# A scan's mixing products and the splitting of its result in two halves, a unit apart in every block; two sums of w_out in another place

## The chip, the cores and the metric

The kernel runs on one core of a Trainium2 chip. The metric is the device time of one execution in microseconds. Smaller is better. The engines are named as the profile names them: PE is TensorE (matmuls), PEld its weight loads, DVE is VectorE, ACT is ScalarE, POOL is GpSimd, SP is SyncE, which issues nearly all DMAs here.

## The reference

A chunked state space scan (4 sequences, 8 heads, 768 tokens, head width 32, state 16), and then a two-layer network with a hard-swish between the layers, over 3072 tokens of width 256, with 2048 hidden units:

```
y_intra = einsum('bhij,bhjd->bhid', (C B^T) * exp(cum_i - cum_j) * causal, x)
y_inter = einsum('bhin,bhnd->bhid', C, state) * exp(cum)
state   = decay_full * state + sum_j decay_from_j * B_j x_j
x2 = y, heads side by side                  # (3072, 256)
h  = x2 @ w_in                              # (3072, 2048)
g  = h * clip(h + 3, 0, 6) / 6
out = g @ w_out                             # (3072, 256)
```

The reference computes the scan in chunks of 32 tokens; the result does not depend on the length of a chunk.

## The kernel before

**Chunks and blocks.** The 768 tokens of each sequence are cut into six chunks of 128; chunk c of the scan gives the 512 tokens (128 of each of four sequences) of block c of the network. The network's block k runs on PE while the scan of chunk c = k + 1 is woven into it, so that chunk c is ready when block c begins. The loop over k at the end of the kernel writes this order out by hand; every engine works through its own queue in the order in which the code issues. Block 0's weights arrive and are decoded during block 0, which therefore has a form of its own (`mlp_in`, `first_out`).

**The network's block.** In blocks 1 to 5 the first product splits operands in three parts: `y` into `high`, `low` and `gap`, w_in into `w_high`, `w_low`, `w_gap`. For each of 16 slices f of the hidden units, `lead` (L687) multiplies `gap` by `w_gap` and has DVE (odd f, L696) or ACT (even f, L699) scale the result in PSUM; `follow` (L701) adds the products of `high` and `low`, and ACT (L706) and DVE (L707) make g of it. `lead` runs two slices ahead of `follow`, and six PSUM banks go round. The second product of blocks 1 to 4 is `wide_units` (L851), a scheme with seven products in place of eight for 2 x 2 quarters, in 14 units of work i = 0 to 13, two for each product. It needs sums of quarters of w_out, made once by `weight_sums` (L750, instructions L761), in the order t3, t2, t4 and t1, and sums of quarters of g, made in every block by POOL (`g_sums`, L769, instructions L779). Units 2 and 3 use t4, units 6 and 7 use t1, units 8 and 9 use t3, units 10 and 11 use t2. At unit 12 the first two `lead`s of the next block are issued. The last block's second product is `out_units`.

**The scan's chunk.** In the same units stand: `scores` (L529) and `multiply` (L573) at unit 2, which give the masked and decayed scores in `L` (DVE, L584), and the state in the middle of the chunk (`mid`); `renew` for the new state; `decay_ends` for the next chunk (ACT, L401, and POOL, L412). Then `results` (L937) issues `mix` (L598) and `split_y` (L666). `mix` multiplies scores by x: for each half u of the heads 64 products on 64 x 32 tiles of the array, each in two passes (128 matmuls for both halves, L610). To these `from_state` (L510) adds the state's part: for each of four sequences and four pairs of heads one product on a 32 x 64 tile, at tile position (32q, 64(q mod 2)) for pair q, in two passes (32 matmuls, L516). `split_y` copies y scaled to `high` (ACT, L671), takes `low` (DVE, L674) and `gap` (DVE, L677).

In which unit this happens depends on the chunk: for chunks 2, 4 and 5 all of it is in unit 6; for chunk 3 (`TURN`) the first half of the mixing is in unit 6, and the second half, the state's part of both halves and `split_y` are in unit 7. Chunk 1 has its place in the second product of block 0, where `first_out(b, i, c)` goes over quarters i of the hidden units and sequences b: scores behind (i, b) = (2, 3), results behind (3, 1), and the first two `lead`s of block 1 inside (3, 3). Chunk 0 is computed before the loop; there alone `from_state` is issued in two halves, for pairs 0 and 1 behind the first half of the mixing and for pairs 2 and 3 behind the second.

After `results` stand, in the same unit, the load of x for the next chunk (`load_x`), the exponential of its decays (`from_start`, ACT L405) and, where there is such a chunk, the loads of the decay rows of the one behind that (`rows`: two DMAs of `L` and four of `eto`, on SP's queue, where the output's stores queue too).

Of the kernel before, what the change touches and what calls it, by code (L numbers as in the profile page):

```python
# [9 lines left out]
FP32R = mybir.dt.float32r  # L10
# [4 lines left out]
ALU = mybir.AluOpType  # L15
# [6 lines left out]
def kernel(  # L22
# [24 lines left out]
    nc = tc.nc  # L47
# [7 lines left out]
    NK = DM // P  # L55
    PC = DM
    NQ = NH // 2
    Z = 2.0 ** -12
    UP = 1.0 + Z
    CUT = 1.0 - Z / 2  # L60
# [26 lines left out]
    TURN = 3  # L87
# [71 lines left out]
    def conceal_in(t, pattern):  # L159
# [26 lines left out]
        out=head, in_=head, pattern=[[-2 * N, NQ], [-N, 2]], compare_op=ALU.is_ge,  # L186
        fill=0.0, base=0, channel_multiplier=1)
    nc.gpsimd.affine_select(
        out=head, in_=head, pattern=[[2 * N, NQ], [N, 2]], compare_op=ALU.is_ge,
# [69 lines left out]
    low = pre[:G, 10, :2 * P]  # L259
# [76 lines left out]
    def y_tile(name, dtype):  # L336
        return att.tile([P, NK, TB], dtype, name=name, tag="y", bufs=3)

    yTs, states, mids, bTs, bss, tmps = {}, {}, {}, {}, {}, {}
    ys, cbs, sps, adds = {}, {}, {}, {}  # L340
# [169 lines left out]
    def from_state(c, a, pairs=range(NQ)):  # L510

        csT, state = bTs[c][2], (mids[c] if a else states[c - 1])
        for b in range(NB):
            for q in pairs:
                pair, d0 = slice(32 * q, 32 * q + 32), 2 * D * (q % 2)
                nc.tensor.matmul(  # L516
                    out=ys[c][a, q // 2][d0:d0 + 2 * D, b], lhsT=state[pair, b],
                    rhs=csT[pair, b, HALF[a]], start=(a == 0 and b == 0), stop=True,
                    tile_position=(32 * q, d0), skip_group_check=True)
# [78 lines left out]
    def mix(c, parts=range(2)):  # L598


        xt = xts[c]
        if 0 in parts:
            ys[c].update({
                (1, u): ps.tile([P, NB, HT], FP32, name="y2", tag=f"f{u}") for u in range(2)})
        for u in parts:
            for b in range(NB):
                for h in range(u * HU, (u + 1) * HU):
                    for a, rows in enumerate(HALF):
                        d0 = D * (h % HU)
                        nc.tensor.matmul(  # L610
                            out=ys[c][a, u][d0:d0 + D, b], lhsT=xt[rows, b * NH + h],
                            rhs=Ls[c][rows, b, h], start=(b == 0 and a >= min(c, 1)), stop=True,
                            tile_position=(a * HT, d0), skip_group_check=True)
            if c == 0:
                from_state(c, 1, (2 * u, 2 * u + 1))
        if c and 1 in parts:
            from_state(c, 1)

    def keep(c):

# [5 lines left out]
    def y_half(t, a, u):  # L626
        return t[:, u].rearrange("p (b i) -> p b i", b=NB)[:, :, HALF[a]]
# [20 lines left out]
    highs, lows, gaps, hs = {}, {}, {}, {}  # L648
# [14 lines left out]
            out=w_part(i, w_gap, j), in0=w_part(i, w_high, j), scalar=1.0 + 1.0 / Z,  # L663
            in1=first_in[i][:, j], op0=ALU.mult, op1=ALU.subtract)

    def split_y(c):  # L666

        highs[c], lows[c], gaps[c] = (y_tile(n, FP32R) for n in ("high", "low", "gap"))
        for u in range(NK):
            for a in range(2):  # L670
                nc.scalar.mul(y_half(highs[c], a, u), ys[c][a, u], CUT)  # L671
        for u in range(NK):
            for a in range(2):
                nc.vector.tensor_tensor(  # L674
                    out=y_half(lows[c], a, u), in0=ys[c][a, u], in1=y_half(highs[c], a, u),
                    op=ALU.subtract)
            nc.vector.scalar_tensor_tensor(  # L677
                out=gaps[c][:, u], in0=lows[c][:, u], scalar=-1.0 / Z, in1=highs[c][:, u],
                op0=ALU.mult, op1=ALU.add)

    def in_product(h, w, y, f, start=False):
        for j in range(NK):
# [250 lines left out]
    def rows(c):  # L933
        load_decay(c)
        load_eto(c)

    def results(c, parts=range(2)):  # L937
        mix(c, parts)
        split_y(c)

    def decay_ends(c, b):
        decay(c, b)
# [13 lines left out]
    parts = {i: decode(i) for i in range(2 * NP)}  # L956

    def weights(i, n):
        for _ in range(n):
            next(parts[i], None)  # L960
# [63 lines left out]
    for k in range(NC):  # L1024
        gTs[k] = ffn.tile([P, NF, TB], FP32, name="gT")
        c, ahead = k + 1, k + 2
        if k == 0:
            for f in range(NF):
                mlp_in(k, f)
                for i in weave.get(f, []):  # L1030
                    weights(i, 1)
                if f in (6, 8):
                    diff_exp(c, f // 2 - 3)
            load_bc(ahead)
            weights(NP + 1, 1)
            weights(NP + 3, 1)
            weights(NP + 2, 3)
            sums = weight_sums()
            for i in range(NP):
                for b in range(NB):  # L1040
                    first_out(b, i, c)
                    if (i, b) == (0, 0):
                        weights(NP + 3, 1)
                        weights(NP + 2, 1)
                        weights(NP + 3, 3)
                        rows(ahead)
                    elif (i, b) == (1, 0):
                        for j in range(NP - 1):
                            high_w(j)
                        for j in range(2):  # L1050
                            low_w(j)
                            gap_w(j)
                    elif (i, b) == (2, 0):
                        turn(c, 1)
                        wake(c)
                        turn(c, 0)
                        low_w(2)
                        gap_w(2)
                        high_w(NP - 1)
                        for p in range(2):  # L1060
                            conceal(ahead, p)
                    elif (i, b) == (2, 3):
                        scores(c)
                        multiply(c)
                        renew(c)
                        decay_ends(ahead, 0)
                        decay_ends(ahead, 1)
                        next(sums)
                        next(sums)
                    elif (i, b) == (3, 1):  # L1070
                        results(c)
                        next(sums)
                        decay_ends(ahead, 2)
                        load_x(ahead)
            rows(ahead + 1)
            continue
        for f in range(NF):
            if f == 0:
                if ahead < NC:
                    load_bc(ahead)  # L1080
                if 1 < k and c < NC:
                    carry(c)
                turns = turn_parts(c) if c < TURN else iter(())
            if f + 2 < NF:
                lead(k, f + 2)
            follow(k, f)
            if k == 1:
                if f in (0, 2):
                    low_w(NP - 1, f // 2)
                if f in (4, 6):  # L1090
                    gap_w(NP - 1, f // 2 - 2)
                if f in (1, 3):
                    decay(c, NB - 1, range(f // 2 * HU, (f // 2 + 1) * HU))
                if f == 3:
                    ends(c, NB - 1)
                    from_start(c)
                    carry(c)
            if f in (4, 8) and ahead < NC:
                conceal(ahead, f // 4 - 1)
            if f in (5, 7, 8):  # L1100
                next(turns, None)
            if f == 9 and c < TURN:
                turn(c, 1)
            if f in (4, 8, 12):
                g_sums(k, f // 2 - 2)
        for i, _ in enumerate((wide_units if c < NC else out_units)(k)):
            if i == 0:
                g_sums(k, NJ - 2)
                if k == 1:
                    next(sums)  # L1110
            if c < NC:
                if i == 1 and c == NC - 1:
                    own_banks(c)
                if i == 2:
                    scores(c)
                    multiply(c)
                    if c < NC - 1:
                        renew(c)
                if ahead < NC and 2 <= i < 6:
                    decay_ends(ahead, i - 2)  # L1120
                if i == 6 and c == TURN:
                    mix(c, (0,))
                if i == (7 if c == TURN else 6):
                    results(c, (1,) if c == TURN else range(2))
                    if ahead < NC:
                        load_x(ahead)
                        from_start(ahead)
                    if ahead + 1 < NC:
                        rows(ahead + 1)
                if i == 9 and TURN <= ahead < NC:  # L1130
                    turn_all(ahead)
                if i == 12:
                    lead(c, 0)
                    lead(c, 1)
# [30 lines left out]
```

## Time and profile before

| | |
|---|---|
| median of three runs | 349.99 us (347.1 to 352.08) |
| the profiled execution | 349.42 us |
| its span, first to last instruction | 347.7 us |
| mean granted clock of TensorE | 0.995 |
| PE busy | 335.3 us, 96% of the span |
| DVE, ACT, POOL busy | 220.1, 173.5, 141.5 us |
| first product, L683, matmuls | 51.8 + 50.7 + 50.3 us |
| mixing products, L610 | 9.8 us in 768 matmuls |
| state's part of y, L516 | 5.1 us (with `mid`) in 192 matmuls |
| sums of w_out, L761 | 1.21, 1.32, 1.21 and 2.22 us |

The span is the time from the first to the last instruction of the program on the core; the execution's own time is 1.7 us more. Rows of the profile give for each line of the code the busy time, the mean length of an instruction in nanoseconds, and the idle time of its engine just before, with what ended it; "issue" there means that no wait for a semaphore was seen. The ends of matmuls are modelled, so the pace of a stream of them is read from where the next ones start. In the timeline a row merges consecutive instructions of one kind and gives the start, the length and the count. In a table by stretches each engine has its busy time and the number of its instructions, and after them stand the granted clock of TensorE, the share of the DMA engines' time and GB/s.

### The profile page before, as it was taken

Reading aid. Unit: us, or ns where it says so; the run is one execution under the profiler, and the core shown is the slowest. Engines: PE = TensorE matmul, PEld = TensorE weight load, DVE = VectorE, ACT = ScalarE, POOL = GpSimd, SP = SyncE. Lnnn points to the kernel's source line nnn. Section 1 sums busy time; section 2 is a strip of 40 time slices with the busy share of each in tenths; the row PEclk is TensorE's granted clock in tenths of the full one; section 3 lists DMA queues with packets and bytes.
Section 4 is the critical chain, followed back from the end, with each engine's and each line's share of the span. In section 5 each row is a group of like instructions: output and inputs, shape, how many; then the busy total and the mean of one; then the engine's idle time right before and its main releaser. Section 6 shows DMA issues by size and latency. Waiting matters only on the chain.

```text
span 347.7 us, 8242 instructions
## 1 busy us (share of the span) xinstructions
PE 335.3 (96%) x3408; PEld 267.8 (77%) x3408; DVE 220.1 (63%) x357; ACT 173.5 (50%) x360; POOL 141.5 (41%) x139
## 2 busy tenths in 40 slices
PE   6799999998999999999999999999999979999996
PEld 2554458887778888888888888888887868888996
DVE  6689999988697648774448674438663332576011
ACT  4768888737874651663741663741662010565000
POOL 3300000291299913299512299510399100089500
PEclk9999999999999999999999999999999989999999
DMA  7898969106930066241047242051200000200000
GB/s 170 160 340 170 248 194 173 33 2 94 198 59 17 5 96 135 34 62 42 2 60 164 35 58 50 4 67 23 34 4 0 2 8 11 32 16 0 2 31 30
DMA packets 91605, 24.89 MB, mean 72 GB/s; under 512 B 84208, under 2 KB 87952, under 8 KB 91056
## 3 DMA queue, kind: packets, MB, share of 16 engines
q1 hardware_dynamic: 87184, 23.06, 34.5%
q10 hardware_dynamic: 4384, 1.31, 1.6%
q8 instruction: 26, 0.43, 0.5%
q14 instruction: 11, 0.09, 0.1%
HBM read 21.07 MB, written 3.29 MB: 70 GB/s over the span
## 4 chain that ended last, share of the span: by engine, by line
PE 89%; DVE 5%; DMA 3%; issue 1%; ACT 1%; SPq 1%; DVEq 0%
PE h L683 31%; PE wb L860 13%; PE wc L860 8%; PE h L635 8%; PE wa L860 8%; PE o L734 6%; PE oa L793 4%; PE ob L793 4%; PE y L610 2%; PE y L516 2%; PE cb L543 2%; DMA raw<-in_moe_w_in_dram 2%; DVE L L584 1%; DMA pairs<-in_C_dram 1%; PE y L555 1%
## 5 line engine op out<-in xcount | busy, mean ns | idle before, releaser
L707 DVE SCALAR_TENSOR_TENSOR gT<-gT,h 128x512 f32<-128x512 f32 x80 | 54.9, 687 | 32.1 <-ACT gT L706 29.3
L706 ACT ACTIVATE gT<-h,half_up 128x512 f32<-128x512 f32 x80 | 55.1, 690 | 33.3 <-PE h L683 33.1
L779 POOL TENSOR_TENSOR s<-gT 128x512 f32<-128x512 f32 x20 | 25.7, 1287 | 69.9 <-DVE gT L707 69.9
L683 PE MATMUL h<-gap,w_gap 128*128 128x512 f32 x160 | 51.8, 409 | 1.0 <-DVE gap L677 1.0
L683 PE MATMUL h<-high,w_high 128*128 128x512 f32 x160 | 50.7, 398 | 0.1
L683 PE MATMUL h<-low,w_low 128*128 128x512 f32 x160 | 50.3, 395 | 0.0
L699 ACT ACTIVATE h<-h 128x512 f32<-128x512 f32 x40 | 23.6, 589 | 31.3 <-PE h L683 31.3
L683 PEld LDWEIGHTS h<-gap,w_gap 128*128 128x128 f32 x160 | 29.9, 188 | 8.0 <-DVE gap L677 1.4
L683 PEld LDWEIGHTS h<-high,w_high 128*128 128x128 f32 x160 | 29.5, 188 | 8.6 <-DVE h L696 2.0
L683 PEld LDWEIGHTS h<-low,w_low 128*128 128x128 f32 x160 | 30.1, 188 | 7.2
L860 PE MATMUL wb<-s,w_out 128*128 128x256 f32 x128 | 32.0, 395 | 0.0
L401 ACT ACTIVATE L<-L,cum_n 128x64 f32<-128x64 f32 x128 | 31.6, 337 | 0.7 <-POOL L L162 0.7
L734 PE MATMUL o<-w_out,gT 128*128 128x256 f32 x128 | 28.7, 381 | 0.0
L696 DVE TENSOR_SCALAR h<-h 128x512 f32<-128x512 f32 x40 | 27.7, 692 | 1.2 <-PE h L683 1.2
L419 POOL TENSOR_TENSOR tmp<-state,eto 128x256 f32<-128x256 f32 x5 | 3.6, 716 | 60.5 <-ACT eto L405 60.3
L635 PE MATMUL h<-yT,w 128*128 128x512 f32 x64 | 27.7, 594 | 0.0
L860 PEld LDWEIGHTS wb<-s,w_out 128*128 128x128 f32 x128 | 24.7, 196 | 3.9
L779 POOL TENSOR_TENSOR s<-s,gT 128x512 f32<-128x512 f32 x20 | 26.9, 1343 | 1.6
L584 DVE TENSOR_TENSOR L<-L,cb 128x512 f32<-128x512 f32 x24 | 15.3, 682 | 19.1 <-PE cb L543 16.3
L734 PEld LDWEIGHTS o<-w_out,gT 128*128 128x128 f32 x128 | 24.1, 190 | 3.8 <-issue 0.5
L412 POOL TENSOR_TENSOR bs<-B,L 128x128 f32<-128x128 f32 x24 | 12.7, 542 | 33.0 <-ACT L L401 27.9
L779 POOL TENSOR_TENSOR gT<-gT 128x512 f32<-128x512 f32 x20 | 25.8, 1291 | 0.0
(141 smaller groups left out, 534.7 us busy)
## 6 DMA issues: line engine op xcount, KB each, us to landing
raw<-in_moe_w_out_dram SPq DMA_DIRECT2D x4, 1024.0 KB
L<-cum_d SPq DMA_DIRECT2D x8, 512.0 KB
xt<-in_x_dram SPq DMA_DIRECT2D x6, 512.0 KB
raw<-in_moe_w_in_dram SPq DMA_DIRECT2D x3, 1024.0 KB
out_dram<-back SPq DMA_DIRECT2D x128, 16.0 KB
eto<-cum_e SPq DMA_DIRECT2D x20, 64.0 KB
B<-in_B_dram SPq DMA_DIRECT2D x5, 256.0 KB
raw<-in_moe_w_in_dram ACTq DMA_DIRECT2D x1, 1024.0 KB
```

The lines of the kernel that those rows point to most:

```text
L401: nc.scalar.activation(Ls[c][:, b, h], Ls[c][:, b, h], AF.Exp, bias=cum_n[:, c, g:g + 1])
L584: nc.vector.tensor_tensor(out=Ls[c][:, :, hs], in0=Ls[c][:, :, hs], in1=cbs[c][q], op=ALU.mult)
L635: nc.tensor.matmul(out=h.rearrange("p r i -> p (r i)"), lhsT=first_in[f // FP][:, j, f % FP * P:(f % FP + 1) * P], rhs=yTs[k][:, j], start ...
L683: nc.tensor.matmul(out=h, lhsT=w[:, j, f * P:(f + 1) * P], rhs=y[:, j], start=(start and j == 0), stop=True, skip_group_check=True)
L696: nc.vector.tensor_scalar(out=h, in0=h, scalar1=-Z / UP, scalar2=None, op0=ALU.mult)
L699: nc.scalar.mul(h, h, -Z / UP)
L706: nc.scalar.activation(g, h, AF.Relu, bias=half_up, scale=UP * UP / 6.0)
L707: nc.vector.scalar_tensor_tensor(out=g, in0=g, scalar=UP, in1=h, op0=ALU.min, op1=ALU.mult)
L734: nc.tensor.matmul(out=o[:, b % 2], lhsT=gTs[0][:, f, b * P:(b + 1) * P], rhs=w_out[:, f], start=(f == 0 and b % 2 == 0), stop=True, skip_ ...
L779: nc.gpsimd.tensor_tensor(out=o, in0=p_, in1=q_, op=op)
L793: nc.tensor.matmul(out=bank[:, slot], lhsT=lhs[:, j], rhs=rhs[:, j], start=(clear and j == 0), stop=True, skip_group_check=True)
L860: nc.tensor.matmul(out=bank[:, slot], lhsT=lhs[:, j], rhs=rhs[:, j], start=(clear and j == 0), stop=True, skip_group_check=True)
```

## The change

- `from_state` for the second half of a chunk is issued in two halves, for pairs 0 and 1 and for pairs 2 and 3, in all chunks and not only in chunk 0, each behind its half of the mixing.
- `split_y` and `results` take one half u at a time.
- Chunks 2 to 5: half 0 (mixing, its state part, its part of `high`, `low` and `gap`) in unit 6, half 1 in unit 7. `load_x`, `from_start` and `rows` follow half 1 in unit 7; for chunk 3 they were there already.
- Chunk 1: half 0 behind (3, 0) of block 0's second product, half 1 behind (3, 1).
- Sums of w_out: before, t3 and t2 were issued behind (2, 3), t4 behind (3, 1) and t1 in unit 0 of block 1. Now t3 is issued behind (3, 1), t2 and t4 behind slices f = 10 and f = 12 of block 1's first product, and t1 in unit 0 as before.

```
@@ mix
-            if c == 0:
-                from_state(c, 1, (2 * u, 2 * u + 1))
-        if c and 1 in parts:
-            from_state(c, 1)
+            from_state(c, 1, (2 * u, 2 * u + 1))
...
-    def split_y(c):
-        highs[c], lows[c], gaps[c] = (y_tile(n, FP32R) for n in ("high", "low", "gap"))
-        for u in range(NK):
-            for a in range(2):
-                nc.scalar.mul(y_half(highs[c], a, u), ys[c][a, u], CUT)
-        for u in range(NK):
-            for a in range(2):
...
+    def split_y(c, u):
+        if u == 0:
+            highs[c], lows[c], gaps[c] = (y_tile(n, FP32R) for n in ("high", "low", "gap"))
+        for a in range(2):
+            nc.scalar.mul(y_half(highs[c], a, u), ys[c][a, u], CUT)
+        for a in range(2):
+            nc.vector.tensor_tensor(
+                out=y_half(lows[c], a, u), in0=ys[c][a, u], in1=y_half(highs[c], a, u),
+                op=ALU.subtract)
+        nc.vector.scalar_tensor_tensor(
+            out=gaps[c][:, u], in0=lows[c][:, u], scalar=-1.0 / Z, in1=highs[c][:, u],
+            op0=ALU.mult, op1=ALU.add)
...
-    def results(c, parts=range(2)):
-        mix(c, parts)
-        split_y(c)
+    def results(c, u):
+        mix(c, (u,))
+        split_y(c, u)
@@ block 0, second product
                         decay_ends(ahead, 0)
                         decay_ends(ahead, 1)
-                        next(sums)
-                        next(sums)
+                    elif (i, b) == (3, 0):
+                        results(c, 0)
                     elif (i, b) == (3, 1):
-                        results(c)
+                        results(c, 1)
                         next(sums)
@@ first product of blocks 1 to 5
+            if k == 1 and f in (10, 12):
+                next(sums)
@@ units of the second product
-                if i == 6 and c == TURN:
-                    mix(c, (0,))
-                if i == (7 if c == TURN else 6):
-                    results(c, (1,) if c == TURN else range(2))
+                if i in (6, 7):
+                    results(c, i - 6)
+                if i == 7:
                     if ahead < NC:
                         load_x(ahead)
                         from_start(ahead)
```

More of the change, by code (lines that the diff above doesn't have):

```diff
@@ L664, in gap_w @@
             in1=first_in[i][:, j], op0=ALU.mult, op1=ALU.subtract)
-    def split_y(c):
-        highs[c], lows[c], gaps[c] = (y_tile(n, FP32R) for n in ("high", "low", "gap"))
-        for u in range(NK):
-            for a in range(2):
-                nc.scalar.mul(y_half(highs[c], a, u), ys[c][a, u], CUT)
-        for u in range(NK):
-            for a in range(2):
[L674 to L679, printed above, removed]
+    def split_y(c, u):
[10 more added lines that the diff above has]
+            op0=ALU.mult, op1=ALU.add)
     def in_product(h, w, y, f, start=False):
```

## The prediction

> **What bounds the kernel now.** I read the page first, then the chain of waits of PE, the stretches by block, and the timeline where PE stands still.
>
> ```profile
> PE 335.3 (96%) x3408; PEld 267.8 (77%) x3408; DVE 220.1 (63%) x357; ACT 173.5 (50%) x360; POOL 141.5 (41%) x139
> q8 instruction: 26, 0.43, 0.5%
> ...
> PE 89%; DVE 5%; DMA 3%; issue 1%; ACT 1%; SPq 1%; DVEq 0%
> ```
>
> PE sets the end: 89% of the last chain, 12.4 us of the span not busy. So a part of the change counts if it alters PE's own time or makes PE wait; work of DVE, ACT or SP counts only where PE runs into it. Blocks 1 to 4, from first output product to first output product, as stretches (length, then busy time and counts of each engine, clock, DMA):
>
> ```profile
> 108.65:160.20 51.55, 51.55 (x530) 43.03 (x529) 35.66 (x54) 25.62 (x64) 31.22 (x29) 1.00 0.37 60
> 160.20:212.13 51.93, 51.93 (x529) 42.99 (x529) 30.75 (x53) 25.62 (x64) 26.97 (x26) 1.00 0.36 60
> 212.13:263.70 51.57, 51.57 (x530) 43.01 (x529) 30.17 (x53) 25.62 (x64) 23.90 (x23) 1.00 0.18 27
> 263.70:319.40 55.70, 53.87 (x531) 44.32 (x530) 26.14 (x45) 17.67 (x31) 20.18 (x17) 0.97 0.07 11
> ```
>
> Three blocks run PE without a pause. The second, which alone splits the mixing already, is 0.37 longer than its neighbours (51.93 - 51.56). The last is 4.1 longer: it holds a pause and a spell of lower clock (0.97).
>
> **The pause in block 4, which the split should remove.**
>
> ```profile
> 280.20 0.69 PE L516 MATMUL y<-csT,mid 32*64 32x64 f32 x30
> 282.72 0.27 PE L516 MATMUL y<-csT,mid 32*64 32x64 f32 x2 [1.83 <-issue]
> ...
> 283.38:286.79 3.41, 3.41 (x10) 2.70 (x9) 1.47 (x3) 0.03 (x1) 0.00 (x0) 0.50 0.09 15
> ```
>
> PE stops before the last two of 32 products, and no semaphore is named ("issue"). The instruction queue q8 moved 0.43 MB in 26 packets, 16.5 KB each; PE's 6816 weight loads and matmuls over 26 are 262 a packet. Counting PE's instructions in the trace, this pause stands before number 6081 and the one at 20.29 us, also "issue", before number 705: 5376 apart, 21 times 256. So I read both as a packet of instructions that came late. Packet 23 started at 279.80 and took 1.47; PE had entered the preceding 256 at 279.01 and went on at 282.72: 3.71 from entering one page to having the next. Mixing plus state products are 320 instructions in 2.1 us, so a page that lies wholly in them is used up too soon. After the pause the clock is 0.50 for 3.41 us (third line), 1.70 lost. Block 4 against block 3 is 4.13 longer; 0.36 of that is that the old state's products stand in a unit of their own there (263.70 to 273.12 against 212.13 to 221.19, 9.42 against 9.06). The pause is thus worth 3.77. After the change a unit of `wb` (1.92) stands inside that page: the rest of the first mixing half 0.37, state half 0.61 (below), `wb` 1.92, second half 0.79, 13 of 32 state instructions 0.25, sum 3.94, over 3.71. I take -3.77; bounds 0 (the packet is later still: packet 10 started 3.07 after its page was entered) and -3.77.
>
> The Trainium skill, Runtime: NRT & Kernel Launch, section Instruction fetch mechanics, has it that the sequencer fetches 16 KiB (256 instructions) ahead and that crossing such a boundary is mostly hidden. The spacing agrees with the trace, the hiding doesn't (1.83 us). By that rule this part would bring nothing, and the sum below would be 355.3 in place of 351.5.
>
> **What the split costs PE.** Two prices, both already in the trace because chunk 0 and block 2 do them.
>
> ```profile
> 20.52 0.68 PE L516 MATMUL y<-csT,mid 32*64 32x64 f32 x16
> 21.13 0.86 PE L610 MATMUL y<-L,xt 64*32 64x64 f32 x64
> ...
> 124.79 0.69 PE L516 MATMUL y<-csT,mid 32*64 32x64 f32 x32
> ...
> 226.87 1.48 PE L610 MATMUL y<-L,xt 64*32 64x64 f32 x128
> 228.28 0.69 PE L516 MATMUL y<-csT,mid 32*64 32x64 f32 x32
> 228.90 1.99 PE L860 MATMUL wb<-s,w_out 128*128 128x256 f32 x8
> ```
>
> One more change from large to small products and back: block 2 shows it, 0.37. Blocks 1, 3, 4 and the end of block 0 get it anew: 4 x 0.37 = 1.48. The state products: chunk 0 issues them in two halves (pairs 0-1, then 2-3), and 16 instructions take from 20.52 to 21.13, 0.61; all 32 with four pairs take 124.79 to 125.41, 0.62. Two pairs use two tile positions where four use four, so a half takes as long as the whole. The change does this to chunks 1 to 5: 5 x 0.60 = 3.00. Bounds 0 (the halves stand between other products and might overlap them; in chunk 0 they don't) and 3.00; I take 3.00, the same line in the same form.
>
> **End of block 0.** Here DVE held PE up: `gap` of chunk 1 comes behind two sums of w_out (1.21 and 1.32).
>
> ```profile
> 82.44 0.53 PE L683 MATMUL h<-gap,w_gap 128*128 128x512 f32 x1
> ...
> 83.97 0.97 PE L683 MATMUL h<-gap,w_gap 128*128 128x512 f32 x3 [1.00 <-DVE gap L677]
> ```
>
> In a stream these products start 0.23 apart; here 1.53, so 1.30 is lost. With the sums gone, DVE is free at 78.4; ACT ends 16 exponentials (L401) at 79.30, then two `high` copies, the output copy (0.56), two more: 81.2. DVE then needs two `low` and a `gap` a half: first `gap` about 81.0, second 82.3. PE gets to them at 82.44 + 0.37 + 0.60 = 83.4. So -1.30, with 1.1 of cover; gone, it would give 1.30 back. The third sum then stands at 82.3 to 83.5, where the next scaling of h (L696) comes behind it as now.
>
> **The two sums in block 1's first product** (t2 and t4, behind the ramps of f = 10 and 12). DVE's order there now, and a sum beside POOL's:
>
> ```profile
> 103.30 0.69 DVE L707 SCALAR_TENSOR_TENSOR gT<-gT,h 128x512 f32<-128x512 f32 x1 [0.52 <-ACT gT L706]
> 103.91 0.69 DVE L696 TENSOR_SCALAR h<-h 128x512 f32<-128x512 f32 x1
> 104.70 0.69 DVE L707 SCALAR_TENSOR_TENSOR gT<-gT,h 128x512 f32<-128x512 f32 x1
> 106.10 0.69 DVE L707 SCALAR_TENSOR_TENSOR gT<-gT,h 128x512 f32<-128x512 f32 x1 [0.71 <-ACT gT L706]
> 106.71 0.69 DVE L696 TENSOR_SCALAR h<-h 128x512 f32<-128x512 f32 x1
> ...
> 110.02 2.22 DVE L761 TENSOR_TENSOR w_out<-w_out 128x1024 f32<-128x1024 f32 x1
> ...
> 111.23 2.13 POOL L779 TENSOR_TENSOR s<-s,gT 128x512 f32<-128x512 f32 x1
> ```
>
> Queued behind t2 is the L696 of f = 13, behind t4 that of f = 15, and PE's last products wait for that one: already now their weight load comes at 107.45, 0.05 after L696 ends, with a wait of 0.22. Inserted are 1.32 + 1.21 = 2.53; DVE has 0.71 + 0.11 free there (before 106.10, and before 104.70). So the last L696, and PE, are 1.71 late: the lower bound. Upper: POOL works without a break from 102.4 to 113.4, and t1, run against it, took 2.22 where its sisters took 1.21 to 1.32, while a POOL sum took 2.13 for 1.28. With 2.22 each: 4.44 - 0.82 = 3.62. A sum may arrive at any point of a POOL instruction, t1 came at the start of one, so I take the middle, 2.7.
>
> The Trainium skill, SBUF — State Buffer, section Who interferes with whom, speaks against this move: a DVE instruction with two SBUF inputs and a GpSimd one that reads SBUF exclude each other for a whole instruction. The t1 row agrees. By the rule at its worst the sum would be 352.4; without it, 350.5.
>
> **At nothing.** `high`, `low` and `gap` come in the same number; the first half is ready earlier, and the products that read them start some 5 us after the second (127.8 to 128.4 `gap`, 135.7 lead). In blocks 1 and 3 the load of x, the exponential of eto and the seven loads of the decay rows issue one unit (some 2.5) later; SP's output stores queue behind them, but x and the decays are read tens of us later, and only the last block's stores, which don't move, touch the end. POOL's sums shift by about 1 to 2; PE reads the last of them (the s of `wb`) 8 us after they are done.
>
> **The sum.** -3.77 + 1.48 + 3.00 - 1.30 + 2.7 = +2.1. On the profiled execution's 349.42 (span 347.7 and 1.7 around it) that is 351.5. That execution lies 0.6 under the median of the runs, 349.99.
>
> **Rivals.** (a) The late page stays late, though the change separates the halves. For: packets started between 0.7 and 3.1 after their page was entered. Against: 3.94 against 3.71, and no window of 256 instructions over the new order is shorter than about 3.8. It gives 351.5 + 3.8 = 355.3. (b) The slower side: semaphores added or taken shift the boundaries by a few instructions, and scores, 320 instructions in 2.4 us, run dry instead (their page 9 arrived about when it was needed: its packet ended at 114.27, PE came at 115.48). Each such pause costs 3.8; with the kept one of block 4 one more gives 359.1. It decides from the second pause on. Against: scores don't change and the boundary lies there only in blocks 1 to 3. (c) The sums hide: if L696 of f = 13 and 15 weren't behind them, +2.7 falls away: 348.8. Against: the order of the queue.
>
> **How the numbers follow.** Forecast 0.50 (own range 350.5 to 352.4), (a) 0.15, (b) 0.15, (c) 0.17, and 0.03 for a gain that no row shows. The range 348.0 to 355.8 takes in the forecast, (c) and (a), 0.82. Over 2% (7 us, about what a measurement of this kernel can tell from no change) are slower: (b), 0.15; faster: 0.03; within: 0.82.
>
> **What would show it.** Right: no "issue" gap near 280 and clock 1.00 there; block 4 near 52.9; blocks 1 and 3 near 52.5, block 2 near 52.5; each half of L516 about 0.6; no wait of L683 for `gap`; PE waiting for L696 at the end of block 1's first product, 1.7 to 3.6. Wrong: an "issue" pause of over 1 us in blocks 1 to 4, halves of L516 at 0.3, or no wait for L696.

## The result, and the profile after

The changed kernel took 352.67 us (median of 12 executions, 351.2 to 356.22), the kernel before 347.9 (12 executions, 347.1 to 352.08): a ratio of 1.0122, 95% interval 1.0088 to 1.0155. It is slower by 1.2%, about 4.2 us by the ratio and 4.8 at the medians, and so within the 2% and the range of the forecast, just above the likeliest case's own range (350.5 to 352.4). The profiled execution of the changed kernel took 351.53 with a span of 349.8, 2.1 us longer than the profiled span before. So two numbers have to be told apart in what follows: 2.1 between two profiled executions, and 4.2 (4.8 at the medians) between the kernels. Differences in us between kernels are by the ratio below, unless the text says otherwise.

In the changed file the lines of the network stand a few numbers lower: L670 and L673 are L674 and L677 before, L679 is L683, L692 is L696, L703 is L707, L757 is L761, L775 is L779, L856 is L860. The stretches of blocks 1 to 4 (length, busy time and counts of each engine, clock, DMA):

```profile
111.11:163.62 52.51, 52.51 (x530) 43.60 (x529) 33.48 (x53) 25.73 (x64) 31.04 (x28) 1.00 0.35 57
163.62:216.16 52.54, 52.54 (x530) 43.54 (x529) 31.05 (x53) 25.85 (x64) 27.40 (x26) 1.00 0.36 61
216.16:268.66 52.50, 52.50 (x529) 43.51 (x529) 30.35 (x53) 25.83 (x64) 24.32 (x23) 1.00 0.17 26
268.66:321.53 52.87, 52.87 (x531) 43.53 (x530) 26.20 (x45) 17.78 (x31) 20.18 (x17) 1.00 0.07 11
```

All four blocks now run PE without a pause and at full clock. Blocks 1 to 3 were 51.55, 51.93 and 51.57 and are 0.96, 0.61 and 0.93 longer; block 4 was 55.70 and is 2.83 shorter. The timeline of PE where the pause had been:

```profile
283.75 0.86 PE L610 MATMUL y<-L,xt 64*32 64x64 f32 x64
284.54 0.68 PE L516 MATMUL y<-csT,mid 32*64 32x64 f32 x16
285.15 1.99 PE L856 MATMUL wb<-s,w_out 128*128 128x256 f32 x8
287.07 0.86 PE L610 MATMUL y<-L,xt 64*32 64x64 f32 x64
287.86 0.68 PE L516 MATMUL y<-csT,mid 32*64 32x64 f32 x16
```

Read from start to start: a half of the mixing (32 products in two passes each, so 64 instructions) takes 0.79, a half of the state products 0.61 (284.54 to 285.15, and 0.61 again at the second half), the unit of `wb` 1.92. PE's 6081st instruction is still inside the second state half, and nothing stops before it.

The end of block 0 (DVE) and the first products that need `gap` (PE):

```profile
80.53 0.69 DVE L673 SCALAR_TENSOR_TENSOR gap<-low,high 128x512 fp32r<-128x512 f32 x1
81.14 0.79 DVE L670 TENSOR_TENSOR low<-y,high 128x256 fp32r<-128x256 f32 x2
81.97 0.69 DVE L673 SCALAR_TENSOR_TENSOR gap<-low,high 128x512 fp32r<-128x512 f32 x1
...
83.48 1.29 PE L679 MATMUL h<-gap,w_gap 128*128 128x512 f32 x4
84.61 1.02 PE L730 MATMUL o<-w_out,gT 128*128 128x256 f32 x4
```

Both gaps are there 0.8 us and more before PE asks for them. From the first product with `gap` to the output products behind the two leads PE now takes 1.13 (83.48 to 84.61), before 2.34 (82.44 to 84.78): 1.21 gained. Those output products in the kernel before, and its first products of block 1's second product:

```profile
84.78 1.02 PE L734 MATMUL o<-w_out,gT 128*128 128x256 f32 x4
...
108.49 1.24 PE L860 MATMUL wa<-gT,w_out 128*128 128x256 f32 x5
```

In the changed kernel, in block 1's first product, DVE, PE and POOL:

```profile
103.72 1.96 DVE L757 TENSOR_TENSOR t<-t,w_out 128x1024 f32<-128x1024 f32 x1
105.59 0.69 DVE L692 TENSOR_SCALAR h<-h 128x512 f32<-128x512 f32 x1
...
107.39 1.86 DVE L757 TENSOR_TENSOR t<-w_out,t 128x1024 f32<-128x1024 f32 x1
109.18 0.69 DVE L692 TENSOR_SCALAR h<-h 128x512 f32<-128x512 f32 x1
...
106.34 0.73 PE L679 MATMUL h<-high,w_high 128*128 128x512 f32 x2 [0.72 <-DVE h L692]
109.92 0.73 PE L679 MATMUL h<-high,w_high 128*128 128x512 f32 x2 [1.45 <-DVE h L692]
110.95 1.24 PE L856 MATMUL wa<-gT,w_out 128*128 128x256 f32 x5
...
104.57 2.23 POOL L775 TENSOR_TENSOR s<-gT 128x512 f32<-128x512 f32 x1
108.13 2.25 POOL L775 TENSOR_TENSOR gT<-gT 128x512 f32<-128x512 f32 x1
```

Each sum is followed by a scaling of h, and each of these two scalings ends about 0.05 before the product of PE that names it as what it waited for. Beside both sums a POOL instruction takes 2.2 where its neighbours take 1.3. From the output products behind the two leads to block 1's second product the kernel before took 23.71 (84.78 to 108.49), the changed one 26.34 (84.61 to 110.95): 2.63 more, of which 2.17 are the two waits named in PE's rows; the rest lies in the starts around them.

### The profile page after: what moved, and what is told of

Read it like the earlier page. It is cut to its first block, busy times and chain, and to the rows that moved or that the text cites. A ratio compares the mean times of both kernels' runs of the same rounds, so it can differ in the third digit from the quotient of the medians.

```text
span 349.8 us, 8240 instructions
## 1 busy us (share of the span) xinstructions
PE 338.1 (97%) x3408; PEld 269.9 (77%) x3408; DVE 219.7 (63%) x357; ACT 174.4 (50%) x360; POOL 145.0 (41%) x139
## 4 chain that ended last, share of the span: by engine, by line
PE 91%; DVE 3%; DMA 3%; ACT 1%; SPq 1%; issue 0%; DVEq 0%
PE h L679 29%; PE wb L856 12%; PE wc L856 8%; PE o L730 8%; PE h L632 8%; PE wa L856 8%; PE oa L789 4%; PE ob L789 4%; PE y L516 3%; PE y L610 3%; PE cb L543 2%; DMA raw<-in_moe_w_in_dram 2%; PE y L555 1%; DMA pairs<-in_C_dram 1%; DVE t L757 1%; ACT gT L702 1%
## 5 line engine op out<-in xcount | busy, mean ns | idle before, releaser
L703 DVE SCALAR_TENSOR_TENSOR gT<-gT,h 128x512 f32<-128x512 f32 x80 | 54.7, 686 | 31.6 <-ACT gT L702 28.9
L775 POOL TENSOR_TENSOR s<-gT 128x512 f32<-128x512 f32 x20 | 26.7, 1334 | 64.1 <-DVE gT L703 64.1
L679 PE MATMUL h<-high,w_high 128*128 128x512 f32 x160 | 50.9, 399 | 2.3 <-DVE h L692 2.2
L679 PE MATMUL h<-gap,w_gap 128*128 128x512 f32 x160 | 51.5, 408 | 0.0
L679 PE MATMUL h<-low,w_low 128*128 128x512 f32 x160 | 50.3, 395 | 0.0
L679 PEld LDWEIGHTS h<-high,w_high 128*128 128x128 f32 x160 | 29.4, 188 | 11.3 <-DVE h L692 4.9
L679 PEld LDWEIGHTS h<-low,w_low 128*128 128x128 f32 x160 | 30.1, 188 | 7.2
L679 PEld LDWEIGHTS h<-gap,w_gap 128*128 128x128 f32 x160 | 30.0, 188 | 6.7
L419 POOL TENSOR_TENSOR tmp<-state,eto 128x256 f32<-128x256 f32 x5 | 4.9, 983 | 65.0 <-ACT eto L405 64.9
L856 PE MATMUL wb<-s,w_out 128*128 128x256 f32 x128 | 30.7, 382 | 0.0
L692 DVE TENSOR_SCALAR h<-h 128x512 f32<-128x512 f32 x40 | 27.6, 691 | 2.2 <-PE h L679 2.2
L775 POOL TENSOR_TENSOR s<-s,gT 128x512 f32<-128x512 f32 x20 | 26.9, 1345 | 1.6
L856 PEld LDWEIGHTS wb<-s,w_out 128*128 128x128 f32 x128 | 24.0, 190 | 3.5
L775 POOL TENSOR_TENSOR gT<-gT 128x512 f32<-128x512 f32 x20 | 26.6, 1330 | 0.0
```

The lines of the kernel that those rows point to most:

```text
L679: nc.tensor.matmul(out=h, lhsT=w[:, j, f * P:(f + 1) * P], rhs=y[:, j], start=(start and j == 0), stop=True, skip_group_check=True)
L692: nc.vector.tensor_scalar(out=h, in0=h, scalar1=-Z / UP, scalar2=None, op0=ALU.mult)
L703: nc.vector.scalar_tensor_tensor(out=g, in0=g, scalar=UP, in1=h, op0=ALU.min, op1=ALU.mult)
L775: nc.gpsimd.tensor_tensor(out=o, in0=p_, in1=q_, op=op)
L856: nc.tensor.matmul(out=bank[:, slot], lhsT=lhs[:, j], rhs=rhs[:, j], start=(clear and j == 0), stop=True, skip_group_check=True)
```

## The experiments

The question after the result was not where the time goes in the profile, which adds up, but whether each cause is the one named, and why the kernels differ by 2 us more than their two profiles. All ratios are to the kernel before, with executions of it on the same chip beside each.

| kernel | median us | ratio to before, 95% interval | profiled span |
|---|---|---|---|
| changed kernel | 352.67 | 1.0122 (1.0088 to 1.0155) | 349.8 |
| before, once more | 348.16 | 0.9995 (0.9962 to 1.0029) | 346.6 |
| before, chunk 5 split | 346.5 | 0.9942 (0.9904 to 0.9980) | 345.7 |
| before, state products in halves | 349.92 | 1.0052 (1.0021 to 1.0083) | 349.3 |
| before, sums moved | 349.99 | 1.0051 (1.0014 to 1.0088) | 348.4 |
| changed, state products whole | 349.5 | 1.0034 (0.9999 to 1.0070) | 347.8 |
| changed, sums put back | 349.33 | 1.0036 (1.0000 to 1.0073) | 347.6 |
| changed, POOL away from the sums | 352.84 | 1.0133 (1.0057 to 1.0210) | 349.4 |
| changed, state products woven in | 358.67 | 1.0301 (1.0257 to 1.0344) | 356.8 |
| before, three findings | 345.77 | 0.9912 (0.9879 to 0.9945) | 344.7 |

**The kernel before, once more.** No edit.

> The kernel before, unchanged, profiled once more. Theory: the pause of about 1.8 us late in block 4 is in every execution, since it comes from where PE's instructions lie, while the spell at half clock behind it (1.7 us) is in some only; so this execution shows the pause near 281 us, and where the clock stays at 1.00 a span near 346.0 against 347.7. Rival: the pause itself is a chance of the first profile; then no pause is seen and the span is near 344.

The pause is there, 1.30 us, at the same two products, with the clock at 1.00 all through block 4. From the chain that ended last, and the stretch of block 4:

```profile
281.40 0.62 PE y L516 x30
282.01 1.30 issue
283.32 0.27 PE y L516 x2
...
264.83:318.30 53.47, 52.16 (x530) 43.13 (x530) 26.11 (x45) 17.68 (x31) 20.21 (x17) 1.00 0.07 11
```

So the theory holds: the pause belongs to the program, the spell at half clock does not. Block 4 was 55.70 in the first profile and is 53.47 here. Of the four profiles that have this pause (the two of before, the halves and the moved sums) two show the spell in block 4 and two don't. The span came out at 346.6, not 346.0: chunk 0 had a pause of its own (1.2 us, "issue", before PE's 705th instruction; 0.47 in the first profile), and block 1 is 0.46 longer with an "issue" pause of 0.32 in its scores, while the pause in block 4 is 0.53 shorter.

**Chunk 5 split, nothing else.**

```
-                if i == 6 and c == TURN:
+                if i == 6 and c in (TURN, NC - 1):
                     mix(c, (0,))
-                if i == (7 if c == TURN else 6):
-                    results(c, (1,) if c == TURN else range(2))
+                if i == (7 if c in (TURN, NC - 1) else 6):
+                    results(c, (1,) if c in (TURN, NC - 1) else range(2))
```

> The kernel before, with chunk 5 alone taken as chunk 3 is: first half of the mixing in unit 6, second half, the undivided state products and the splitting of y in unit 7. Theory (a late instruction packet): one more unit of 1.9 us stands inside the packet's 256 instructions, the time from entering it to its end is 0.37 + 1.92 + 0.79 + 0.44 = 3.5 us against 3.7 needed, so the pause shrinks from 1.8 to 0.2 us or less and the clock stays at 1.00; the price is 0.37 for the switch of forms. Against a kernel before without the clock spell about 1.3 us faster, against one with it 3. Rival (the pause belongs to something else, such as a wait for mid or a bank): the pause stays and the time rises by 0.4 us.

```profile
265.15:317.43 52.28, 52.28 (x531) 43.00 (x530) 26.12 (x45) 17.56 (x31) 20.18 (x17) 1.00 0.07 11
```

No pause is left; block 4 is 1.19 shorter than in the profile just shown, the 0.37 for the split included. The pause is so worth 1.56 in the execution without the clock's spell and 3.79 in the one with it (53.47 and 55.70, each less 52.28 - 0.37). The 2.23 between them are 0.53 of a longer pause (1.83 against 1.30) and 1.70 of the spell. The kernel is faster than before by 0.6%, clear of its interval. A wait for mid or for a bank would have stayed, as no operand changed its producer.

**State products in halves, nothing else.**

```
-            if c == 0:
-                from_state(c, 1, (2 * u, 2 * u + 1))
-        if c and 1 in parts:
-            from_state(c, 1)
+            from_state(c, 1, (2 * u, 2 * u + 1))
```

> The kernel before, with the state products issued in two halves (pairs 0-1 behind the first half of the mixing, pairs 2-3 behind the second) in every chunk, all of it still in one unit. Theory: a half costs what the whole costs, so chunks 1 to 5 cost 0.6 us more each; in block 4 the longer section eats 0.6 of the pause, and block 1's gap waits are behind it by 0.6 less; so blocks 1 to 3 are 0.6 longer each, the whole about 1.8 slower. Rival: the halves overlap the mixing around them and the blocks keep their length within 0.1.

```profile
160.71:213.23 52.52, 52.52 (x529) 43.52 (x529) 31.23 (x53) 25.84 (x64) 27.41 (x26) 1.00 0.36 59
213.23:265.55 52.32, 52.32 (x529) 43.61 (x529) 30.16 (x53) 25.85 (x64) 24.36 (x23) 1.00 0.18 26
265.55:321.02 55.47, 54.62 (x530) 44.91 (x530) 26.14 (x45) 17.79 (x31) 20.19 (x17) 0.97 0.07 11
```

Block 2 is 0.59 longer; block 3 is 0.75 longer, since with both halves in one unit the mixing is cut as well (one change of form more; its price follows with the woven kernel). Block 1 (52.59) is 1.04 longer, of which 0.15 is a short pause in its scores. The rival is out. In block 4 the pause fell to 0.85, as the section is longer, and a spell at half clock stands behind it all the same, where none stands behind 1.30 in two other profiles; what brings the spell isn't shown. In time 0.5% slower, as expected.

**The changed kernel with the state products whole**, behind the first half of the mixing. For the second half of the heads they then open the sum:

```
@@ from_state
-                    rhs=csT[pair, b, HALF[a]], start=(a == 0 and b == 0), stop=True,
+                    rhs=csT[pair, b, HALF[a]], stop=True,
+                    start=(b == 0 and (a == 0 or (c > 0 and q >= 2))),
...
@@ mix
-                            rhs=Ls[c][rows, b, h], start=(b == 0 and a >= min(c, 1)), stop=True,
+                            rhs=Ls[c][rows, b, h], stop=True,
+                            start=(b == 0 and a >= min(c, 1) and (c == 0 or u == 0)),
...
-            from_state(c, 1, (2 * u, 2 * u + 1))
+            if c == 0:
+                from_state(c, 1, (2 * u, 2 * u + 1))
+            elif u == 0:
+                from_state(c, 1)
```

> The changed kernel, but with the state products undivided behind the first half of the mixing (for the second half of the heads they then open the sum, and the mixing adds to it). Theory: blocks 1 to 4 are 0.6 us shorter each, block 0's end too, where the cover of the gap shrinks from 0.8 to 0.2; in block 4 the packet has 0.37 + 0.62 + 1.92 + 0.79 less what lies behind its end, about 3.5, so a pause of up to 0.3 can come back. In all 2.7 to 3.0 us faster than the changed kernel. Rival: if halves cost nothing where they stand, the blocks keep 52.5.

```profile
111.52:163.42 51.90, 51.90 (x529) 42.99 (x529) 33.55 (x53) 25.72 (x64) 30.62 (x28) 1.00 0.36 58
267.29:319.56 52.27, 52.27 (x530) 43.00 (x530) 26.13 (x45) 17.66 (x31) 20.18 (x17) 1.00 0.07 11
```

Each block is 0.6 shorter than in the changed kernel (52.51 and 52.87), and no pause came back. Against before the ratio falls from 1.0122 to 1.0034, 0.9% or 3 us: the halves cost what they were said to cost.

**The state products woven into the mixing**, four behind each sequence's sixteen mixing products. This asks why a half is so dear.

```
@@ from_state
-    def from_state(c, a, pairs=range(NQ)):
+    def from_state(c, a, pairs=range(NQ), bs=range(NB)):
...
-        for b in range(NB):
+        for b in bs:
...
@@ mix, inside the loop over b and then behind it
+                if c:
+                    from_state(c, 1, (2 * u, 2 * u + 1), (b,))
-            from_state(c, 1, (2 * u, 2 * u + 1))
+            if c == 0:
+                from_state(c, 1, (2 * u, 2 * u + 1))
```

> The changed kernel, with the state products of each half issued sequence by sequence between the mixing products (four of each half's sixteen behind each sequence's mixing) and not behind them all. Theory: a half costs as much as the whole because its products use only two tile positions of the array and each waits for the one before at its position; with mixing products in between the positions have time to come free, so most of the 0.30 us that a half pays too much goes: blocks 1 to 4 become 0.3 to 0.6 us shorter each, the kernel 1.5 to 2.5 faster than the changed one. Rival: what a half pays too much is the change of form from mixing to state products and back; woven there are four of these changes in each half, and the blocks become longer.

The kernel becomes longer, as the rival said. The first half of one of its halves, from the chain that ended last:

```profile
126.99 0.27 PE y L610 x16
127.26 0.26 PE y L516 x4
127.52 0.27 PE y L610 x16
127.80 0.26 PE y L516 x4
```

A quarter of the mixing takes 0.27 where it took 0.20 (0.79 for four), and four state products 0.26 where they took 0.15. Instruction by instruction, PE's last matmul of one form starts at 235.017 and the first weight load of the other form at 235.161: 0.144 without a start, at each change of form. Within the state products the starts come in rounds of 0.058, two instructions a round with two pairs and four with four. So a half of 16 is 0.144 and eight rounds, the whole of 32 is 0.144 and eight rounds too, both 0.61. The theory had the rounds right and put the change of form at nothing; woven, a half has six changes more. Of the 0.60 that the two halves of the changed kernel pay over the whole, 0.144 is the one extra change, the rival's reason, and 0.46 the half-empty rounds, the larger part.

**The sums moved, nothing else** (t3 behind `results`, t2 and t4 behind f = 10 and 12):

```
-                        next(sums)
-                        next(sums)
...
+            if k == 1 and f in (10, 12):
+                next(sums)
```

> The kernel before, with the sums of w_out where the change puts them (t3 behind (3, 1) of block 0, t2 and t4 behind f = 10 and 12 of block 1's first product) and nothing else. Theory: the wait for gap at the end of block 0 goes (-1.3 us), DVE's two sums hold up the scalings behind them and PE waits 0.7 and 1.5 us (2.4 in all by the changed kernel's profile): 1.1 us slower, with the pause of block 4 as before. Rival: those waits come from the later arrival of the split halves, so without the split they aren't there and the kernel is 1.3 faster.

PE waits for the scalings 2.2 us in all, as in the changed kernel, though the mixing is not split here; the rival is out. The wait for `gap` did not go wholly: from the first product with `gap` to the output products behind it takes 1.41 (83.63 to 85.04), 0.28 more than in the changed kernel; here both gaps come behind one unit that holds all of the mixing. The time is 0.5% above before, 1.8 us, where 1.1 was expected. The profile adds up to 1.7: 0.93 gained there (2.34 to 1.41), 2.65 lost in block 1's first product (23.71 to 26.36).

**The changed kernel with the sums put back.** The same edit, reversed.

> The changed kernel, with the sums of w_out where they were before (t3 and t2 behind (2, 3), t4 behind (3, 1)). Theory: block 1's first product loses its waits (-2.4 us), and at the end of block 0 a wait of 0.4 to 0.6 for gap returns, less than the 1.0 of before since PE comes 1.0 later: about 1.9 faster than the changed kernel. Rival: if the sums only fill idle time of DVE in block 1, this kernel is slower than the changed one by the returned wait.

From the first `lead` to block 1's second product it takes 24.74 (84.05 to 108.79), in the changed kernel 27.28 (83.83 to 111.11). Of the wait for `gap` only 0.1 returns where 0.4 to 0.6 were expected; 1.17 us of DVE's time before `low` are idle in the changed kernel, and the sums fill these first. The ratio is 1.0036 in place of 1.0122.

**POOL away from the sums.**

```
-            if f in (4, 8) and ahead < NC:
+            if f in ((4,) if k == 1 else (4, 8)) and ahead < NC:
...
-            if f in (4, 8, 12):
+            if f in ((4,) if k == 1 else (4, 8, 12)):
                 g_sums(k, f // 2 - 2)
...
                 g_sums(k, NJ - 2)
                 if k == 1:
+                    conceal(ahead, 1)
+                    g_sums(k, 2)
+                    g_sums(k, 4)
```

> The changed kernel, with POOL's sums of g for f = 4 to 11 of block 1 and the second masking of the next chunk issued behind the last sum of the first product, so that POOL stands still while DVE makes t2 and t4. Theory (DVE and POOL hold each other up): t2 and t4 take 1.3 and 1.2 us in place of 1.96 and 1.87, and PE's waits shrink by 1.2 to 1.3 us. Rival: the sums are long for another reason (where their operands lie); they stay at 1.9 and nothing is gained.

```profile
104.45 1.22 DVE L757 TENSOR_TENSOR t<-t,w_out 128x1024 f32<-128x1024 f32 x1
107.38 1.22 DVE L757 TENSOR_TENSOR t<-w_out,t 128x1024 f32<-128x1024 f32 x1
...
111.99 2.18 POOL L775 TENSOR_TENSOR s<-gT 128x512 f32<-128x512 f32 x1 [8.96 <-DVE gT L703]
...
109.26 0.73 PE L679 MATMUL h<-high,w_high 128*128 128x512 f32 x2 [0.80 <-DVE h L692]
```

With POOL idle for 8.96 us both sums take 1.22, and PE's waits fall from 0.72 and 1.45 to none and 0.80: the stretch from the first `lead` is 1.36 shorter (25.92 against 27.28). So the length of the sums is due to POOL working beside them. The ratio shows none of it: 1.0133, from four executions and with an interval of 1.5%. Two of the four ran at a mean clock of 0.999 and took 350.20 and 351.18, where the changed kernel's five executions at full clock took 351.20 to 352.58; that is the expected way, but two are few. In its profile block 1 is 0.25 longer (52.76 against 52.51) and chunk 0 has a pause of 1.4 that the changed kernel's profiled execution doesn't have. For the time this run stays inconclusive; for the cause it is clear.

**Three findings in the kernel before**: chunk 5 split with whole state products, chunk 3 not split, t2 behind the splitting of y beside t4.

```
-                if i == 6 and c == TURN:
+                if i == 6 and c == NC - 1:
-                if i == (7 if c == TURN else 6):
-                    results(c, (1,) if c == TURN else range(2))
+                if i == (7 if c == NC - 1 else 6):
+                    results(c, (1,) if c == NC - 1 else range(2))
...
                         decay_ends(ahead, 1)
                         next(sums)
-                        next(sums)
...
                         results(c)
                         next(sums)
+                        next(sums)
```

> The kernel before, with three of the findings: only chunk 5 is split over two units, with undivided state products (pause of block 4 gone: -1.3 to -3); chunk 3 is not split any more (-0.37 if the packets allow it; if they don't, a pause near 178 us); and one sum, t2, is moved from before the splitting of y of chunk 1 to behind it, beside t4 (-1.3, the wait for gap, with the scaling behind t4 where it was). In all about 3 us faster than the kernel before, near 345. Rival: the two sums together delay block 1's first scaling and PE waits there instead, so only the pause is gained: 346.3.

```profile
161.01:212.57 51.56, 51.56 (x529) 42.99 (x529) 30.95 (x53) 25.63 (x64) 27.57 (x26) 1.00 0.38 62
264.14:316.42 52.28, 52.28 (x530) 43.00 (x530) 26.12 (x45) 17.58 (x31) 20.18 (x17) 1.00 0.07 11
```

Blocks 2 and 4 have their shorter forms without a pause, and of the wait for `gap` 0.28 is left, read as in the moved sums (1.41, 83.66 to 85.07). It is faster than the kernel before by 0.9% (0.9912, interval 0.9879 to 0.9945), 3.1 us by the ratio as expected, 2.2 at the medians. Its profile also has an "issue" pause of 0.39 in block 1's scores.

## Why the prediction was right

It forecast a change within 2%, slightly to the slower side, for reasons that offset each other; the runs bear out each reason, and the size of one term was off. The terms beside what the two profiles and the runs show:

| term | predicted | measured |
|---|---|---|
| change of form in blocks 1, 3 and at the end of block 0 | 0.37 each | with the halves 0.96 and 0.93 |
| state products in halves | 0.60 each | 0.61 in block 2; whole again: 0.61, 0.62, 0.55, 0.60 shorter |
| wait for gap, end of block 0 | -1.30 | -1.21, with 0.8 of cover (predicted 1.1) |
| t2 and t4 in block 1's first product | +2.7 (1.7 to 3.6) | +2.63 (23.71 to 26.34) |
| pause of block 4 | -3.77 | -3.79 in the profiled execution, -1.56 where the clock holds |
| sum, between profiled executions | +2.1 | +2.1 (span 347.7 to 349.8) |

By stretches of PE the two profiles differ by +0.16 up to the last products of chunk 1's scores (L555, from 73.39 and 73.55), -0.33 from there to the output products behind the first two leads (forecast 0.37 + 0.60 - 1.30 = -0.33), +2.63 to block 1's second product, and -0.33 in blocks 1 to 4 (forecast -0.26). Behind that they don't differ.

**The late packet.** The count was 3.94 us from the first instruction of the page to its end against 3.71 needed; no pause is left, and the experiment with chunk 5 alone shows that one unit between the halves is what removes it. The 3.71 was one execution's figure: in the four profiles with this pause a packet of q8 starts 0.80 to 0.87 after PE entered the preceding 256 instructions, takes 0.94 to 1.47, and PE goes on 1.41 to 1.45 after its end, so 3.2 to 3.7 in all. The pause is longest where the packet took longest (1.83 with 1.47 in the first profile, 1.30 with 0.94 in the second). The five pauses before the 705th instruction end 1.36 to 1.51 after the end of a packet, and three short ones in block 1's scores 1.29 to 1.41. This ties the pauses to the packets; no run changed the fetching itself. The rule of the Trainium skill that a boundary is mostly hidden (Runtime: NRT & Kernel Launch, Instruction fetch mechanics) did not hold for this section in either profile of the kernel before (1.83 and 1.30 us). Rival (a) is out. Of rival (b) a small form exists: scores run dry in block 1 in three profiles (0.32 in the second one of the kernel before, 0.15 with the halves, 0.39 with the three findings), though not in the changed kernel's, and it costs 0.5 us at most where the rival had 3.8.

**The term that was mis-sized** is this pause's, -3.77. It was read from one execution, with the longer packet and with the spell at half clock; the second profile has neither, and there the pause is worth 1.56. At -1.56 in place of -3.77 the sum is +4.3, and the kernels differ by 4.2 by the ratio. Executions that had no spell anywhere can be set beside each other: with a mean clock of 0.998 or more the changed kernel's five have a median of 352.11; of the kernel before, 18 of 35 in one series beside the experiments have 347.70 and 16 of 29 in another 347.59. That is 4.4 to 4.5 us. The excess over 2.1 is there where no spell plays a part, and the smaller worth of the pause accounts for it. How often the spell comes in block 4 can't be read from executions without a profile: the other 17 of the 35 have a median of 350.7, but a spell in chunk 0 lowers the mean clock as well. That the two profiles differ by 2.1, just as forecast, is in part luck: the forecast and this comparison start from the same execution with the spell. The forecast time suffers less, since its base, 349.42, holds the spell (it lies 1.5 above the median of twelve, 347.9) and the -3.77 takes it off again: 351.5 is 0.6 under the 352.11.

**The sums.** Both waits stand where the queue's order put them, and rival (c) is out. The middle of the two bounds, 2.7, is 0.07 above the 2.63 measured; it was a choice between 1.7 and 3.6, so its coming so near is luck. The price of the wait for `gap` was read 0.1 too high: the prediction took 0.23 between the first two products with `gap`, and without a wait they start 0.42 apart in the changed kernel. The second place where a page of the Trainium skill was weighed (SBUF — State Buffer, Who interferes with whom: a DVE instruction with two SBUF inputs and a POOL instruction that reads SBUF get in each other's way) held up: with POOL idle the same instructions took 1.22 in place of 1.96 and 1.87.

**Work put at nothing** cost nothing that shows: blocks 1 and 3, where loads and the exponential move by a unit, are 0.96 and 0.93 longer, what 0.37 and 0.60 make.

## What to carry to other kernels

Where one engine is busy 96% of the time, price a reordering on that engine's own starts: a change of form between small tiled products and large ones, and a group of products cut so that it uses half the tile positions, cost PE time even though no instruction is added. A pause that names no semaphore is worth counting instructions for: if it stands a whole number of pages from another one, put slow instructions between the fast ones there, in that place only; doing so everywhere paid four times for what was needed once. And read a price from more than one profiled execution before it carries a sum, above all if a spell of lower clock is a part of it.

## What the runs showed of the hardware

- Between two forms of small tiled matmuls PE started nothing for 0.144 us; within the state products it started one round every 0.058 us, of two instructions where two pairs were issued and of four where four were.
- Mixing and state products ran through 256 instructions in about 1.7 us, while 3.2 to 3.7 passed from entering one 256 to having the next, in the four profiles with the pause. In all twelve pauses named above PE went on 1.3 to 1.5 us after the end of a packet of q8.
- A pause of PE of 0.85 us was followed by 3.41 us at half clock in one profile and one of 1.83 us in another; one of 1.30 us was followed by none in two others.
- Two sums of DVE took 1.96 and 1.87 us with POOL working beside them and 1.22 with POOL idle.
- In chunk 0 PE paused before its 705th instruction ("issue", 0.3 to 1.4 us) in the five profiles whose clock was full there, and not in the six with a spell of half clock before that place.
